# Attention scan, Fourier mixing and two MLPs on one core: the mixing works inside the tile of keys and queries

## The chip, the cores and the metric

One core of a Trainium2 chip runs the whole program. The metric is the device time of one execution in microseconds (us), as a median over runs.

## The reference

For each of 4 images (the batch), 8 heads, 768 positions and a head width of 48, an attention with a complex decaying state is computed, its real part is the image X (768 positions by 384 features), and two MLP blocks follow:

```
for t in range(S):
    S = a_n[t] * S + k[t] v[t]^T          # complex S, a_n = a scaled to |a| <= 0.999
    y[t] = q[t] @ real(S)
u  = X + real(fft(fft(X, axis=positions), axis=features))
un = (u - mean(u)) / sqrt(var(u) + 1e-6)  # per position
u  = u + relu(un @ w_ch1) @ w_ch2         # 384 -> 1536 -> 384
u  = u + (relu(u.T @ w_tok1) @ w_tok2).T  # 768 -> 256 -> 768
out = u + relu(u @ w_ch1') @ w_ch2'       # 384 -> 1536 -> 384
```

## The kernel before

Work on an image b falls into a **chain** (`stage1` and `stage2`) and a **dense** part (the MLPs). The chain of image b+1 runs beside the dense part of image b, so that for b = 0 there is no dense work to run beside, and the chains of images 1, 2 and 3 lie over the dense parts of images 0, 1 and 2. After the chain of image 3 only dense work is left.

- **Scan.** The decay products of the positions are built (DVE, ACT, POOL), and keys and queries, scaled by them, are transposed on PE and copied by ACT (`st_t`, L463 and L641) into a tile `qkt` of 112 partitions by 12288 columns: 64 column groups of 96 for the keys, 64 for the queries. The group of head h and chunk c is h*8+c.
- **Chunks.** The 768 positions are handled in 8 chunks of 96. For chunk c, `ch_load` (L747) fetches the values V and the plain keys Kn, `ch_sc` (L756) makes the masked scores (PE L761, DVE L768), `ch_u` (L771) advances the state: PE L776 and L777, then DVE L787 (Aa), DVE L793, POOL L794 and L795, and DVE L797 (T). `ch_y` (L802) makes the output (PE L810 from scores and values, PE L816 from queries and T), and ACT (L818) puts it into `xT`, 96 columns a chunk. The state update of chunk c-1 gives the T that L816 of chunk c reads; the last update is that issued in chunk 6.
- **Mixing** (`stage2`, L968). It takes a second tile `ws` out of the same pool slot as `qkt` (one buffer), so it begins when the last reader of `qkt` is done. The columns of `ws` are shared out by the table `WSP` (L964). *Folds* (L996) subtract and add column n and column 384+n of `xT`, DVE the difference and POOL the sum; L1002 adds and subtracts halves of these. The table `XP` (L38) says in which column pieces: for b > 0 the pieces are 288 and 96 columns wide. *Mirrors* (L1013) combine column n with column 384-n, with two one-column copies on ACT (L1020, `NR` L39 is the range). Then come a transform over the features (PE L1036, evicted by ACT L1038 into `Z`, first kt = 0 and then kt = 1, four kinds each), the transform over the positions (PE L1047, ACT L1055, L1056 and L1083, POOL L1084 and L1085), transposes (PE L1094) and a join with X (DVE L1099) into `u`, mean and variance (L1106 and L1107), and the normalisation (L1115 to L1122, ACT L1126 writes `un`).
- **Dense.** `transposed` (L907) transposes `un` on PE (L914) and splits it into a high and a low part (ACT L917, DVE L918); `mlp` (L921) runs PE L934 (first matrix), ACT L938 (relu, high part), DVE L947 or ACT L944 and POOL L945 (low part), PE L956 (second matrix) and DVE L959 (adds to `u`). The token MLP is L1145, L1146, L1161, L1167, L1168, L1179 and L1181. For b = 0 the weights are split into high and low parts in the free time of the chain (`tick`: DVE L194, POOL L196, DVE L199, ACT L205, POOL L206).

The order on each engine is set ahead of time: a scheduler plays the program through on a modelled timeline, and where several instructions could go next it takes the one of the better rank. The ranks (`RANK`, L60) put the chain before the dense part on PE, and the dense part before the chain on DVE. The engines then run their lists strictly in this order. The fold of b = 0 is tied by hand to the ticks of chunks 5 and 6.

## Time and profile before

| | before |
|---|---|
| runs | 1093.06, 1094.05, 1094.24 us (median 1094.05) |
| the profiled execution | 1093.5 us; span of its records 1091.7 us |
| PE busy | 978.8 us (90%) |
| DVE / ACT / POOL busy | 769.3 / 511.1 / 417.9 us |
| mean granted clock of PE | 0.966 |

Time is read against the span: 1.8 us of the profiled execution lie outside it. A row of a timeline gives a start, a length, an engine, a line, what is written from what is read, and a count; brackets at its end say how long the engine had been idle before it and what ended that. Rows of neighbouring instructions of one line are taken together, and their lengths overlap a little on PE. A share of busy time over the whole span says little here, since stages differ: the first 180 us are the chain of image 0 alone, the last 260 us are dense work alone.

### The profile page before, as it was taken

The numbers are of one execution on the slowest core, as the hardware profiler recorded it, in microseconds if no ns is written. First come the engines' busy times: TensorE is split into PE (matmuls) and PEld (weight loads), VectorE is DVE, ScalarE is ACT, GpSimd is POOL, SyncE is SP. The second block draws the span as 40 slices with busy tenths as digits, with TensorE's granted clock in tenths as the row PEclk, the third lists the DMA queues.
The fourth block names the chain that finished last, engine by engine and source line by source line (L and its number), as shares of the span: only waits on it lengthen the run. The fifth ranks groups of instructions, "written<-read, shape, count | busy, mean of one in ns | idle before, by whom it ended". The sixth has DMA issues, their size and how long they took to land.

```text
span 1091.7 us, 21067 instructions
## 1 busy us (share of the span) xinstructions
PE 978.8 (90%) x7314; PEld 915.3 (84%) x7314; DVE 769.3 (70%) x2083; ACT 511.1 (47%) x1425; POOL 417.9 (38%) x541
## 2 busy tenths in 40 slices
PE   1567788999899988999998999999897999999997
PEld 0337766989788986899997899999787999999997
DVE  6988887999999678999658879974734433433332
ACT  6753446777875236877216556842224112121111
POOL 6625994673676454345336312424512002000000
PEclk9988896999999999899999999999998999999999
DMA  6238943776668563465575345665303434543432
GB/s 219 48 101 233 290 165 118 252 264 206 200 235 270 162 180 113 117 184 175 156 198 148 100 139 187 203 165 132 128 17 117 146 114 135 159 156 127 163 101 76
DMA packets 101537, 174.66 MB, mean 160 GB/s; under 512 B 11056, under 2 KB 61104, under 8 KB 100912
## 3 DMA queue, kind: packets, MB, share of 16 engines
q1 hardware_dynamic: 101424, 173.24, 51.5%
q8 instruction: 60, 0.98, 0.4%
q14 instruction: 53, 0.43, 0.1%
HBM read 133.88 MB, written 39.32 MB: 159 GB/s over the span
## 4 chain that ended last, share of the span: by engine, by line
PE 68%; DVE 16%; DMA 6%; POOL 4%; ACT 3%; issue 2%; SPq 0%; POOLq 0%; DVEq 0%; ACTq 0%
PE l L956 24%; PE l L934 23%; PE s L761 4%; DMA cvt<-wL 3%; PE s L650 2%; PE s L1047 2%; PE s L810 2%; DVE cvt L199 2%; DVE ws L1002 2%; PE s L1036 1%; PE s L816 1%; PE s L1161 1%; POOL cvt L196 1%; DVE ws L996 1%; PE s L1179 1%
## 5 line engine op out<-in xcount | busy, mean ns | idle before, releaser
L956 PE MATMUL l<-w,h 128*128 128x384 f32 x1728 | 326.5, 339 | 6.8 <-DVE h L947 4.0
L934 PE MATMUL l<-th,w 128*128 128x384 f32 x1152 | 316.0, 344 | 8.8 <-DVE h L947 4.3
L956 PEld LDWEIGHTS l<-w,h 128*128 128x128 f32 x1728 | 297.2, 188 | 11.1 <-DVE h L947 6.3
L934 PEld LDWEIGHTS l<-th,w 128*128 128x128 f32 x1152 | 213.1, 191 | 12.2 <-DVE h L947 6.1
L934 PE MATMUL l<-tl,w 128*128 128x384 f32 x576 | 196.3, 341 | 3.6 <-DVE tl L918 3.6
L938 ACT ACTIVATE h<-l 128x384 fp32r<-128x384 f32 x192 | 94.1, 490 | 213.2 <-PE l L934 212.7
L959 DVE TENSOR_TENSOR u<-u,l 128x384 f32<-128x384 f32 x192 | 105.3, 549 | 83.1 <-PE l L956 82.4
L947 DVE SCALAR_TENSOR_TENSOR h<-l,h 128x384 fp32r<-128x384 f32 x160 | 88.5, 553 | 91.0 <-ACT h L938 90.8
L934 PEld LDWEIGHTS l<-tl,w 128*128 128x128 f32 x576 | 110.3, 191 | 4.2 <-DVE tl L918 4.2
L196 POOL TENSOR_TENSOR cvt<-cvt 128x384 int32<-128x384 int32 x56 | 66.3, 1190 | 38.3 <-DVE cvt L194 7.3
L761 PE MATMUL s<-qkt 112*96 112x96 f32 x512 | 57.8, 263 | 11.0 <-DVE sc L768 11.0
L472 PE MATMUL s<-misc,y 128*112 128x128 f32 x96 | 22.2, 379 | 47.3 <-DVE y L450 44.5
L761 PEld LDWEIGHTS s<-qkt 112*96 112x96 f32 x512 | 51.8, 173 | 13.8 <-DVE sc L768 12.0
L472 PEld LDWEIGHTS s<-misc,y 128*112 128x112 f32 x96 | 14.8, 183 | 57.0 <-POOL tm L366 19.1
L1146 POOL TENSOR_TENSOR xl<-u,xh 128x384 fp32r<-128x384 f32 x18 | 17.9, 1005 | 107.1 <-ACT xh L1145 107.1
L206 POOL TENSOR_TENSOR w<-cvt,w 128x384 fp32r<-128x384 f32 x44 | 52.2, 1197 | 8.3 <-ACT w L205 8.0
L199 DVE SCALAR_TENSOR_TENSOR cvt<-cvt 128x384 int32<-128x384 int32 x56 | 45.9, 828 | 5.9 <-POOL cvt L196 5.8
L579 POOL TENSOR_TENSOR tm<-tm 128x144 f32<-128x144 f32 (+1 forms) x51 | 26.8, 526 | 58.9 <-ACT tm L578 58.6
L945 POOL TENSOR_TENSOR h<-full,h 128x384 fp32r<-128x384 f32 x32 | 33.8, 1057 | 37.2 <-ACT full L944 35.4
L623 DVE TENSOR_TENSOR p<-p,A 128x144 f32<-128x144 f32 x144 | 44.6, 310 | 2.1
L650 PE MATMUL s<-misc,y 128*112 128x128 f32 x288 | 45.2, 276 | 0.9 <-DVE y L634 0.3
L794 POOL TENSOR_TENSOR yc<-Aa,gm 48x384 f32<-48x384 f32 x18 | 21.0, 1164 | 62.4 <-DVE Aa L787 62.4
(232 smaller groups left out, 1940.8 us busy)
## 6 DMA issues: line engine op xcount, KB each, us to landing
w<-wscr SPq DMA_DIRECT2D x180, 384.0 KB, 3.4
cvt<-wL SPq DMA_DIRECT2D x56, 384.0 KB, 5.0
wscr<-w SPq DMA_DIRECT2D x44, 384.0 KB, 3.7
Kn<-kn SPq DMA_DIRECT2D x64, 192.0 KB, 3.7
kn<-y SPq DMA_DIRECT2D x96, 96.0 KB, 2.6
raw<-aL SPq DMA_DIRECT2D x48, 144.0 KB, 3.1
xx<-xL SPq DMA_DIRECT2D x48, 144.0 KB, 2.9
V<-vL SPq DMA_DIRECT2D x32, 144.0 KB, 3.2
```

The source lines that it names most:

```text
L196: x = ge.tensor_tensor(out=a, in0=a, in1=lo, op=ALU.add)
L199: rest(ve.scalar_tensor_tensor(out=a, in0=hi, scalar=-0x80000000, in1=a, op0=ALU.bitwise_and, op1=ALU.bitwise_or))
L206: ge.tensor_tensor(out=parts[:, 1, :], in0=a.bitcast(F32), in1=r32(parts[:, 0, :]), op=ALU.subtract)
L472: te.transpose(ps[:, j, :], y[:, j, 0:112], ident)
L623: ve.tensor_tensor(out=cur, in0=prev, in1=A[:, j, 0:3, :], op=ALU.mult)
L650: te.transpose(ps[:, j, :], y[:, j, 0:112], ident)
L761: te.matmul(out=ps[:, j, :], lhsT=K[:, hc, :], rhs=Q[:, hc, :])
L934: te.matmul(out=ps, lhsT=w1[:, wi, kt * 128:kt * 128 + 128], rhs=x[g][:, kt, :], start=(n == 0), stop=(n == 8))
L938: x = se.activation(out=hi, in_=ps, func=ACTF.Relu)
L947: ve.scalar_tensor_tensor(out=lo, in0=ps, scalar=0.0, in1=r32(hi), op0=ALU.max, op1=ALU.subtract)
L956: te.matmul(out=ps, lhsT=hs[m][:, hi, tt * 128:tt * 128 + 128], rhs=w2[:, wi, :], start=(n == 0), stop=(n == 8))
L959: ve.tensor_tensor(out=u[tt], in0=u[tt], in1=ps, op=ALU.add)
```

## The change

- `qkt` has 128 partitions and its column groups are ordered by chunk: c*8+h for h*8+c. The ACT copies of `st_t` write the same elements in a pattern of one more dimension; `ch_sc` and `ch_y` index accordingly. So the columns of a chunk's keys lie together, and so do those of its queries.
- `stage2` no longer takes a tile of its own: it works in `qkt` (that of b = 0 too, whose folds lay in other tiles before), and its instructions wait for the readers of just the columns that they overwrite. `WSP` puts the halves of the folds (`xd`) over the keys of chunks 0 to 3, the mirrors (`fd`) after it, the folds over queries. Folds are stored closely packed, a piece at a time.
- For b > 0 the pieces of the folds are 192, 96 and 96 columns. The first needs the chunks 0, 1, 4 and 5, the second also 2 and 6, the third also 3 and 7.
- The mirrors are done in two ranges, columns 97 to 192 and then 0 to 96. The order is: folds but the last, mirrors 97 to 192, `dft(1)` (the transform over features with kt = 1), last fold, mirrors 0 to 96, for b = 0 the ticks, `dft(0)`. Only the last fold, its mirrors and `dft(0)` depend on chunk 7.
- For each b > 0 DVE has one fold, three halves and six mirrors more, POOL one fold, one half and two mirrors more, of smaller tiles and the same elements in all; b = 0 has eight more mirrors on DVE.
- `ch_load` of chunk 7 no longer fetches the plain keys, which nothing read (two transfers an image).

```diff
...
 AH = 4
 KS, EN = 5, 3
 OFF = ((2, 3), 1, 0)
-XP = [((0, 96), (96, 96), (192, 96), (288, 96))] + [((0, 288), (288, 96))] * 4
-NR = [((0, 192),)] * 5
-KT, PF, PD = (0, 1), ((2, 0), (2, 1)), (((1, 0), (1, 1)), ((1, 1),))
+XP = [((0, 96), (96, 96), (192, 96), (288, 96))] + [((0, 192), (192, 96), (288, 96))] * 4
+NR = ((97, 192), (0, 96))
+PF, PD = ((2, 0), (2, 1)), (((1, 0), (1, 1)), ((1, 1),))
 O = (0, 1, 0)
 HOLD = mybir.DependencyInfo(mybir.DependencyClass.NoSync, mybir.DependencyReason.SCHED_ONLY)
 CHK_A, CHK_E = 6.0e4, 1.0e-7
...
 
         def st_t(i, k):
             if not qk:
-                qk.append(alloc("qk", [112, 12288], name="qkt").rearrange("p (k g s) -> p k g s", k=2, g=64))
-            qkt = qk[0]
+                qk.append(alloc("qk", [128, 12288], name="qkt"))
+            qkt = qk[0][0:112]
             d = t[i]
             s0 = d["s0"]
             y = ybuf[k][i % 2]
             ps = palloc("s", [112, N4, 128])
             for j in range(N4):
                 te.transpose(ps[:, j, :], y[:, j, 0:112], ident)
-            src = ps.rearrange("p s (g c) -> p g c s", g=2)
+
+            def rows(ap, o, step, g=()):
+                return with_ap(ap, o, [*g, (96, 8), (768, 8), (step, N4)])
+
+            def cols(o, g=()):
+                return with_ap(ps, o, [*g, (8, 8), (1, 8), (128, N4)])
             if k == 0:
-                se.copy(out=with_ap(qkt, s0, [(64 * 96 + 48, 2), (96, 64), (1, N4)]), in_=src)
+                se.copy(out=rows(qkt, s0, 1, [(64 * 96 + 48, 2)]), in_=cols(0, [(64, 2)]))
             else:
-                se.copy(out=with_ap(qkt, 64 * 96 + 47 - s0, [(96, 64), (-1, N4)]), in_=src[:, 0])
-                se.copy(out=qkt[:, 0, :, 48 + s0:48 + N4 + s0], in_=src[:, 1])
+                se.copy(out=rows(qkt, 64 * 96 + 47 - s0, -1), in_=cols(0))
+                se.copy(out=rows(qkt, 48 + s0, 1), in_=cols(64))
 
         def st_end():
 
...
             ve.tensor_scalar(out=gate[:, b:b + 1], in0=fl, scalar1=127.5, scalar2=None, op0=ALU.is_ge)
 
         st = {}
+
+        def halves():
+            v = qk[0][0:112].rearrange("p (k g s) -> p k g s", k=2, g=64)
+            return v[:, 0], v[:, 1]
         PU = "l" if b == 0 else "s"
 
         def ch_load(c):
             v = alloc("P", [96, 384], name="V")
             sp.dma_start(out=v, in_=vL[b, c])
+            st[c] = dict(v=v)
+            if c == 7:
+                return
             kt = alloc("A", [96, 8, 128], name="Kn")
             for hf in range(2):
                 sp.dma_start(out=kt[48 * hf:48 * hf + 48],
                              in_=knd[hf].rearrange("(h c) s f -> c s h f", c=8)[c])
-            st[c] = dict(v=v, kt=kt)
+            st[c]["kt"] = kt
 
         def ch_sc(c, half):
             ps = palloc("s", [96, 4, 96])
-            Q, K = qk[0][:, 1], qk[0][:, 0]
+            K, Q = halves()
             for j in range(4):
-                hc = (half * 4 + j) * 8 + c
+                hc = c * 8 + half * 4 + j
                 te.matmul(out=ps[:, j, :], lhsT=K[:, hc, :], rhs=Q[:, hc, :])
             sc = alloc("e", [96, 4, 96], name="sc")
             mb = mask.unsqueeze(1).to_broadcast([96, 4, 96])
...
 
         def ch_y(c):
             d = st[c]
-            Q = qk[0][:, 1]
+            Q = halves()[1]
             ps = palloc(PU, [112, 4, 96])
             for p in range(4):
                 for k in range(2):
...
                         h = 2 * p + k
                         m = 48 if k else 64
                         te.matmul(out=ps[64 * k:64 * k + m, p, :], lhsT=st["T"][:, h * 48:h * 48 + m],
-                                  rhs=Q[:, h * 8 + c, :], start=False, stop=True)
+                                  rhs=Q[:, c * 8 + h, :], start=False, stop=True)
             marked(se.activation(out=xT[:, :, c * 96:c * 96 + 96], in_=ps, func=ACTF.Copy, scale=gate[0:112, b:b + 1]))
 
         if b == 0:
...
             if b == 0 and c < 7:
                 rests[0], rests[1] = tops[c], st["yop"]
                 tick(CF[c + 1], c == 5)
+        return qk[0]
 
 
     def fallback(b):
...
                     done(tt)
 
 
-    WSP = {"xf": (0, 3072), "Z": (0, 1552), "xr": (1552, 1536), "fd": (3088, 3088), "cb": (3088, 1737),
-           "xd": (6176, 3072), "un": (6176, 2304), "smat": (9248, 2048), "cc": (4825, 1158)}
+    WSP = {"xd": (0, 3072), "fd": (3072, 3088), "xf": (6160, 3072), "Z": (6160, 1552), "xr": (7712, 1536),
+           "smat": (9248, 2048), "cb": (0, 1737), "cc": (1737, 1158), "un": (3072, 2304)}
     ZK = ((128, 64), (128, 64), (128, 65), (128, 63))
 
-    def stage2(b):
-        space = alloc("qk", [128, 12288], name="ws")
+    def stage2(b, space):
         def part(name, pat=None, **kw):
             o, n = WSP[name]
             v = space[:, o:o + n]
...
         u = [alloc("u", [128, 384], name=f"u{i}") for i in range(6)]
 
 
-        if b == 0:
-
-            xm, xp = (alloc("h", [112, 4, 384], name="xf") for _ in range(2))
-            xd = alloc("h", [112, 4, 384], name="xd")
-            xd = [[xd[:, 0:2], xd[:, 2:4]], [alloc("tmp", [112, 2, 384], name="xd") for _ in range(2)]]
-        else:
-            xf = part("xf", "p (a b) -> p a b", a=8)[0:112]
-            xm, xp = xf[:, 0:4, :], xf[:, 4:8, :]
-            xd = part("xd", "p (s r a b) -> p s r a b", s=2, r=2, a=2)[0:112]
-            xd = [[xd[:, s, r] for r in range(2)] for s in range(2)]
+        xd = part("xd", "p (s r a b) -> p s r a b", s=2, r=2, a=2)[0:112]
+        xd = [[xd[:, s, r] for r in range(2)] for s in range(2)]
         fd = part("fd", "p (t r a b) -> p t r a b", t=4, r=2, a=2)[0:112]
         Z = part("Z", "p (a b) -> p a b", a=8)
-        for k, (o, n) in enumerate(XP[b]):
+        kinds = ((0, 0, ALU.subtract, 0, 191), (1, 0, ALU.add, 1, 192), (2, 1, ALU.add, 0, 192), (3, 1, ALU.subtract, 1, 191))
+
+        def folds(k, o, n):
+            at = WSP["xf"][0] + 8 * o
+            x = space[0:112, at:at + 8 * n].rearrange("p (a b) -> p a b", a=8)
             n += o
             an = None if b or AN[k] is None else free[AN[k]]
-            for s, x, op in ((0, xm, ALU.subtract), (1, xp, ALU.add)):
-                x1 = (ge if s else ve).tensor_tensor(out=x[:, :, o:n], in0=xT[:, :, o:n], in1=xT[:, :, 384 + o:384 + n], op=op)
+            for s, op in ((0, ALU.subtract), (1, ALU.add)):
+                y = x[:, 4 * s:4 * s + 4]
+                x1 = (ge if s else ve).tensor_tensor(out=y, in0=xT[:, :, o:n], in1=xT[:, :, 384 + o:384 + n], op=op)
                 if an is not None:
                     after(x1, an)
                 if b == 0 and k == 3 and s == 0:
-                    warm(1, xm[:, 0, :])
+                    warm(1, y[:, 0, :])
                 for r, op2 in enumerate((ALU.add, ALU.subtract)):
-                    x1 = (ge if (s, r) in PD[b > 0] else ve).tensor_tensor(out=xd[s][r][:, :, o:n], in0=x[:, 0:2, o:n], in1=x[:, 2:4, o:n], op=op2)
+                    x1 = (ge if (s, r) in PD[b > 0] else ve).tensor_tensor(out=xd[s][r][:, :, o:n], in0=y[:, 0:2], in1=y[:, 2:4], op=op2)
                     if an is not None:
                         after(x1, an)
                     if b == 0 and k == 3 and s == 0:
                         warm(1, xd[0][r][:, 0, :])
 
-        kinds = ((0, 0, ALU.subtract, 0, 191), (1, 0, ALU.add, 1, 192), (2, 1, ALU.add, 0, 192), (3, 1, ALU.subtract, 1, 191))
-        for n0, n1 in NR[b]:
+        def mirrors(n0, n1):
             for ty, s, op, f0, f1 in kinds:
                 lo, hi, sh = max(n0, f0, 1), min(n1, f1, 191) + 1, ty % 2
                 for r in range(2):
                     x = (ge if (ty, r) in PF and b else ve).tensor_tensor(out=fd[:, ty, r, :, lo - sh:hi - sh], in0=xd[s][r][:, :, lo:hi],
                                                                 in1=xd[s][r][:, :, 384 - lo:384 - hi:-1], op=op)
-                    if b == 0 and ty < 2:
+                    if b == 0 and ty < 2 and not n0:
                         warm(1, fd[:, ty, r, 0, 1:191])
                 for n in (0, 192):
                     if n0 <= n <= n1 and f0 <= n <= f1:
                         for r in range(2):
                             se.copy(out=fd[:, ty, r, :, n - sh:n - sh + 1], in_=xd[s][r][:, :, n:n + 1])
-
-        if b == 0:
-            marked(x)
-            rests[0], rests[1] = x, None
-            for _ in range(5):
-                tick(0)
-            rests[0] = None
-
-
-        for kt in KT:
+            return x
+
+        def dft(kt):
             for ty in range(4):
                 n0, n = 128 * kt, ZK[ty][kt]
                 ps = palloc("s", [128, 2, 97])
...
                         te.matmul(out=ps[0:n, r, :], lhsT=fd[:, ty, r, dt, n0:n0 + n], rhs=dcos[0:112, ty % 2, dt, r, :],
                                   start=(dt == 0), stop=(dt == 1))
                 se.copy(out=Z[0:n, 2 * ty + kt, :].rearrange("p (i r) -> p r i", r=2), in_=ps[0:n])
+
+        for k, (o, n) in enumerate(XP[b][:-1]):
+            folds(k, o, n)
+        mirrors(*NR[0])
+        dft(1)
+        folds(len(XP[b]) - 1, *XP[b][-1])
+        x = mirrors(*NR[1])
+        if b == 0:
+            marked(x)
+            rests[0], rests[1] = x, None
+            for _ in range(5):
+                tick(0)
+            rests[0] = None
+        dft(0)
 
         if b == 0 and WZ:
             warm(WZ, ident)
...
         return f(*args)
 
     def chain(b):
-        stage1(b)
-        return stage2(b)
+        return stage2(b, stage1(b))
 
     sp.dma_start(out=dcos, in_=cD)
     sp.dma_start(out=fk, in_=cFk)
...
     with tc.If(fv != 0):
         with tc.For_i(0, B, 1) as b:
             fallback(b)
-            u, norm = stage2(B)
+            u, norm = stage2(B, alloc("qk", [128, 12288], name="ws"))
             t = transposed(u, norm, "s")
             dense2(B, u, *dense1(B, u, *t), row=b)
 
```

The second `st_t`, for b > 0, is changed in the same way. In the lists that follow, the new kernel's lines are its own: L787 is L804, L793 to L797 are L810 to L814, L768 is L785, L934 is L952, L945 is L963, L947 is L965, L956 is L974, L959 is L977, L914 is L932, L917/L918 is L935/L936, L996 is L1010, L1002 is L1016, L1013 is L1026, L1047 is L1067, L1094 is L1114, L1099 is L1119 and L1161 is L1181.

DVE's list at the end of the chunks of image 3 (u is the dense part's sum; Aa, Xx and T belong to the state update of chunk 6; ws and qkt are the workspace), before:

```order
L787 TENSOR_TENSOR Aa<-T,s 112x384
L793 TENSOR_TENSOR Xx<-Aa,gm_82 112x384
L797 TENSOR_TENSOR T<-Xx,yc_79 112x384
L768 TENSOR_TENSOR sc<-s,misc 96x384 x2
L959 TENSOR_TENSOR u_6497<-u_6497,l 128x384
L996 TENSOR_TENSOR ws<-xT 112x4x288
L996 TENSOR_TENSOR ws<-xT 112x4x96
L959 TENSOR_TENSOR u_6498<-u_6498,l 128x384
L1002 TENSOR_TENSOR ws<-ws 112x2x288 x2
```

And of the changed kernel:

```order
L1010 TENSOR_TENSOR qkt<-xT 112x768
L804 TENSOR_TENSOR Aa<-T,s 112x384
L1016 TENSOR_TENSOR qkt<-qkt 112x2x192 x2
L810 TENSOR_TENSOR Xx<-Aa,gm_82 112x384
L1016 TENSOR_TENSOR qkt<-qkt 112x2x192
L977 TENSOR_TENSOR u_6499<-u_6499,l 128x384
L814 TENSOR_TENSOR T<-Xx,yc_79 112x384
L785 TENSOR_TENSOR sc<-s,misc 96x384 x2
L977 TENSOR_TENSOR u_6500<-u_6500,l 128x384
L1010 TENSOR_TENSOR qkt<-xT 112x384
L1016 TENSOR_TENSOR qkt<-qkt 112x2x96 x3
L1026 TENSOR_TENSOR qkt<-qkt 112x2x95 x6
```

All folds stood behind the last scores; now the fold of 768 elements stands ahead of the state update of chunk 6 and its halves (112x2x192) among it, and the second piece with its mirrors ahead of the third.

POOL's list at the same place (yc is its part of the state update, h the low part of the dense relu), before:

```order
L794 TENSOR_TENSOR yc_79<-Aa,gm_82 48x384
L795 TENSOR_TENSOR yc_79<-Aa,gm_82 48x384
L996 TENSOR_TENSOR ws<-xT 112x4x288
L996 TENSOR_TENSOR ws<-xT 112x4x96
L1002 TENSOR_TENSOR ws<-ws 112x2x288
L1002 TENSOR_TENSOR ws<-ws 112x2x96
L945 TENSOR_TENSOR h<-full,h 128x384
```

And of the changed kernel:

```order
L811 TENSOR_TENSOR yc_80<-Aa,gm_82 48x384
L812 TENSOR_TENSOR yc_80<-Aa,gm_82 48x384
L1010 TENSOR_TENSOR qkt<-xT 112x768
L811 TENSOR_TENSOR yc_79<-Aa,gm_82 48x384
L812 TENSOR_TENSOR yc_79<-Aa,gm_82 48x384
L1016 TENSOR_TENSOR qkt<-qkt 112x2x192
L1010 TENSOR_TENSOR qkt<-xT 112x384
L1016 TENSOR_TENSOR qkt<-qkt 112x2x96
```

POOL's fold of the first piece now stands ahead of its two instructions of chunk 6's state update.

PE's list at the end of image 3's mixing, from the last part of the transform over positions to the token MLP of image 3 (the dense part is that of image 2 up to L956, un of image 3 is in ws or qkt), before:

```order
L1047 MATMUL s<-ws 128x193
L1094 MATMUL s<-misc,xT 128x112 x4
L1094 MATMUL s<-misc,ws 128x112 x4
L956 MATMUL l<-w,h 128x384 x9
L914 MATMUL s<-misc,ws 128x128 x18
L1161 MATMUL s<-xh,w 128x384 x10
```

And of the changed kernel:

```order
L952 MATMUL l<-th,w 128x384 x2
L952 MATMUL l<-tl,w 128x384
L952 MATMUL l<-th,w 128x384
L974 MATMUL l<-w,h 128x384 x6
L932 MATMUL s<-misc,qkt 128x128 x3
L974 MATMUL l<-w,h 128x384 x12
L932 MATMUL s<-misc,qkt 128x128 x6
L974 MATMUL l<-w,h 128x384 x18
L932 MATMUL s<-misc,qkt 128x128 x3
L974 MATMUL l<-w,h 128x384 x18
L932 MATMUL s<-misc,qkt 128x128 x6
L1181 MATMUL s<-xh,w 128x384 x10
```

Behind the last L1094 stood nine matmuls of dense work and then the 18 transposes of `un`; now 10 matmuls of L952 (the list shows the last four) and 54 of L974 stand behind it, and the transposes are spread among them.

## Rows read from the trace of the kernel before

**Rows 1.** The page, busy time of each engine.

```profile
PE 978.8 (90%) x7314; PEld 915.3 (84%) x7314; DVE 769.3 (70%) x2083; ACT 511.1 (47%) x1425; POOL 417.9 (38%) x541
```

**Rows 2.** Windows: stretch, length, busy us (instructions) of PE, PEld, DVE, ACT, POOL, clock, DMA.

```profile
397.00:444.00 47.00, 35.50 (x215) 29.03 (x212) 41.85 (x124) 28.39 (x89) 23.19 (x32) 0.89 0.42 131
444.00:577.00 133.00, 133.00 (x1211) 127.92 (x1210) 105.08 (x323) 74.21 (x224) 55.41 (x82) 0.99 0.59 170
577.00:592.00 15.00, 10.39 (x65) 9.79 (x61) 14.84 (x17) 7.94 (x22) 13.38 (x10) 0.89 0.66 194
775.00:789.00 14.00, 10.42 (x68) 9.36 (x64) 13.23 (x12) 3.54 (x8) 11.47 (x7) 0.99 0.54 188
822.00:834.00 12.00, 5.16 (x23) 4.62 (x24) 6.99 (x16) 6.33 (x16) 5.76 (x6) 0.72 0.23 85
```

**Rows 3.** Timeline of PE, images 1 to 3, the long waits.

```profile
404.69 1.86 PE L956 MATMUL l<-w,h 128*128 128x384 f32 x9 [3.02 <-DVE h L947]
...
583.47 0.45 PE L934 MATMUL l<-tl,w 128*128 128x384 f32 x1 [3.58 <-DVE tl L918]
...
787.18 0.44 PE L934 MATMUL l<-th,w 128*128 128x384 f32 x1 [3.17 <-DVE u L959]
...
829.91 1.54 PE L914 MATMUL s<-misc,ws 128*128 128x128 f32 x6 [6.34 <-ACT ws L1126]
```

**Rows 4.** Timeline of DVE and POOL, image 0, end of its folds.

```profile
138.27 6.20 DVE L1013 TENSOR_TENSOR ws<-xd 112x382 f32<-112x382 f32 x8
...
144.82 8.25 POOL L196 TENSOR_TENSOR cvt<-cvt 128x384 int32<-128x384 int32 x6 [2.16 <-DVE cvt L194]
...
161.92 0.52 POOL L1084 TENSOR_TENSOR ws<-ws 128x193 f32<-128x193 f32 x1
```

**Rows 5.** Timeline of ACT, DVE and POOL, image 1, chunk 6 and the folds.

```profile
390.11 0.58 ACT L818 ACTIVATE xT<-s,gate 112x384 f32<-112x384 f32 x1 [1.18 <-PE s L816]
...
391.03 0.55 DVE L787 TENSOR_TENSOR Aa<-T,s 112x384 f32<-112x384 f32 x1 [1.15 <-PE s L777]
...
391.73 1.15 POOL L794 TENSOR_TENSOR yc<-Aa,gm 48x384 f32<-48x384 f32 x1 [3.83 <-DVE Aa L787]
...
393.82 0.56 DVE L797 TENSOR_TENSOR T<-Xx,yc 112x384 f32<-112x384 f32 x1 [1.65 <-POOL yc L795]
...
397.50 3.82 POOL L996 TENSOR_TENSOR ws<-xT 112x1152 f32<-112x1152 f32 x1 [3.71 <-PE s L816]
...
398.71 3.03 DVE L996 TENSOR_TENSOR ws<-xT 112x384 f32<-112x384 f32 x1
```

**Rows 6.** Groups by form, all images (columns as in the page's list of groups).

```profile
L996 DVE TENSOR_TENSOR ws<-xT 112x1152 f32<-112x1152 f32 x3 | 4.1, 1358 | 3.4 <-PE s L816 3.4
L959 DVE TENSOR_TENSOR u<-u,l 128x384 f32<-128x384 f32 x192 | 105.3, 549 | 83.1 <-PE l L956 82.4
```

**Rows 7.** Timelines of image 1 behind the folds: last mirrors, last eviction.

```profile
412.02 1.35 DVE L1013 TENSOR_TENSOR ws<-ws 112x382 f32<-112x382 f32 x2
...
420.52 0.32 ACT L1038 COPY ws<-s 63x194 f32<-63x194 f32 x1
```

**Rows 8.** Windows behind two of PE's waits (columns as in rows 2).

```profile
583.50:586.00 2.50, 2.50 (x9) 2.50 (x10) 2.50 (x3) 0.80 (x3) 2.50 (x3) 0.58 0.78 183
...
830.00:834.00 4.00, 4.00 (x17) 3.90 (x18) 1.11 (x2) 1.41 (x3) 0.00 (x0) 0.62 0.02 4
```

**Rows 9.** Timelines of PE and ACT: a run of L956 in image 1, then the end of image 3's mixing.

```profile
398.39 3.28 PE L956 MATMUL l<-w,h 128*128 128x384 f32 x18
...
818.98 0.64 PE L1094 MATMUL s<-misc,ws 112*128 112x112 f32 x4
819.39 1.81 PE L956 MATMUL l<-w,h 128*128 128x384 f32 x9
...
831.10 2.91 PE L1161 MATMUL s<-xh,w 128*128 128x384 f32 x10
...
829.15 1.30 ACT L1126 ACTIVATE ws<-u,rs 128x384 f32<-128x384 f32 x2 [3.05 <-DVE rs L1122]
```

More of the change, by code (lines that the diff above doesn't have):

```diff
@@ L642, in st_t @@
             if not qk:
-                qk.append(alloc("qk", [112, 12288], name="qkt").rearrange("p (k g s) -> p k g s", k=2, g=64))
-            qkt = qk[0]
+                qk.append(alloc("qk", [128, 12288], name="qkt"))
+            qkt = qk[0][0:112]
             d = t[i]
```

11 lines of the change are left out of this document (7 added, 4 removed).

## Prediction

> **What bounds the kernel now.** I read the page first: PE is busy for 978.8 us of the span of 1091.7 us [rows 1], so the kernel can only become faster where PE waits or where its clock is low. Then windows by stage: in 444 to 577 us, chunks beside dense work, PE has no gap at all. The gaps sit where the chain runs out of cover, at each image's mixing: 11.5 us of 47 for image 1, 4.6 of 15 for image 2, 3.6 of 14 at the folds of image 3, and 6.8 of 12 before its token MLP [rows 2]. The page by lines would hide this, since the same lines run gapless in other stages. Third, PE's timeline names the long waits. Three stand behind the folds: 3.02 us for L947, 3.58 for L918, 3.17 for L959 [rows 3]; none of these is a fold. They are small dense instructions of DVE that stand in its list behind folds. The fourth, 6.34 us, is for `un` of image 3 [rows 3].
>
> Why the folds hold DVE is in the form and in the neighbour. The first fold, 1152 elements, takes 1.36 us on DVE; the second, a third of it, takes 3.03 us, while POOL's fold of 1152 runs for 3.82 us beside it [rows 5, 6]. L959, which reads one operand from PSUM, is steady at 0.55 us beside anything [rows 6]. So folds on DVE and POOL pass through one gate in turn, whichever came first. The Trainium skill, SBUF — State Buffer, section "Who interferes with whom", has this as a rule: a DVE instruction with two SBUF inputs contends with a GpSimd instruction that reads SBUF, and the one that issued first blocks the other for its whole length. By it, work moved forward beside POOL's does not become free, it blocks what stands behind it; that is the slow rival below, and rows 5 bear the rule out for the folds themselves.
>
> **The change, part by part.** All sums go against the profiled execution, 1093.5 us; the median of the runs, 1094.05, lies 0.55 above it.
>
> *Layout and the copies of the scan.* The ACT copies write the same elements, in one dimension more. No row of before shows that pattern. Nothing speaks for a gain, and ACT is busy for 511.1 of 1091.7 us [rows 1], so I take nothing; if each of the 180 copies took a tenth of a microsecond more, 18 us spread over four scans would have to fit into 580 us of idle ACT. The two transfers a chunk that go are off SP's queue in the last chunk, where nobody waits for them: nothing.
>
> *Image 0, later by 1.2 us.* The mirrors become 16 halves for 8 wholes, which now take 6.20 us [rows 4]. The same elements, eight fixed costs more; two forms give the size of one: 1152 elements in 1.36 us against L959's 384 in 0.55 [rows 6] are 0.81 us for 768 elements, so 0.40 for 384, which leaves about 0.15 us a piece, together 1.2. POOL's conversions start right behind the mirrors (L196 at 144.82), and the mixing's L1084 stands behind their whole queue, at 161.92 [rows 4], so the delay passes to the mixing, which here has no dense work beside it. The split also lets `dft(1)` go early, but `dft(0)` is behind the ticks as before. Bounds: 0, if the shorter pieces slip between POOL's, and 2.5, if each pays double beside POOL.
>
> *Image 1, nothing.* The fold of 768 elements moves ahead of chunk 6's state update. By rows 5 and 6 it costs DVE 0.9 us alone and POOL 2.5 (3.82 by two thirds). POOL sat idle for 3.83 us before L794 [rows 5], but not at the right time: chunk 5's output is in `xT` at 390.69, 0.34 us before L787 [rows 5], so the fold fills the time in which L794 and L795 ran. On DVE three halves of 384 elements stand between L787 and L797 as well. I put chunk 6's T later by POOL's 2.5 us and some 0.6 for halves that wait in turn: 3.1 us. What is saved behind chunk 7 is these same instructions, 4 to 5 us, so that the 3.02 us wait shrinks; but PE gets to chunk 7's end 3 us later. At the other end `Z` is complete with the last L1038 at 420.52 [rows 7]. With kt = 1 first only 12 matmuls remain behind the last mirrors at 413.37 [rows 7], yet in the new list the last L1038 stands behind three more scan instructions of image 2. I let these cancel. Bounds: -4 (all of the wait and the end of the mixing move up) and +3 (T's delay uncovered).
>
> *Image 2, later by 2.5 us.* Here the output of chunk 7 has only six transposes L914 ahead of it as cover when T is late by 3.1 us, so some 2.5 of them reach PE. The wait of 3.58 us for L918 [rows 3] shrinks as the folds leave, but L947 in the new list comes only after all mirrors 97 to 192 and the last fold. Its low clock, 0.58 behind the wait [rows 8], stays as it is. Bounds: -3 and +5.
>
> *Image 3, earlier by 7 us.* This is the change's one large effect, and it is in PE's list: 64 dense matmuls stand behind the last L1094, where nine stood. Eighteen of L956 take 3.28 us, nine 1.81 [rows 9], so 64 are some 11 us, against 9.2 us from the end of the last L1094 (819.62) to `un` at about 829 [rows 9, 3]. The 6.34 us then hold work, and the short waits around it too: 6.8 us idle in this window. PE's clock at 0.62 behind it for 4 us [rows 8] costs some 1.2 us more, since the ten L1161 take 2.91 us there. That makes 8. Against it: the 55 matmuls come from somewhere earlier, between chunk 7 and L1047, where they covered the folds; with T late by 3.1 and a thinner cover I give 1 us back. Bounds: -9, all of it and half the wait of 3.17 at the folds, and -2, where the earlier stage takes most of it back.
>
> Sum: 1.2 + 0 + 2.5 - 7 = -3.3 us, 1090.2 in the profiled execution, 1090.8 as a median.
>
> **The rivals.**
> - *The early folds are free.* Chunk 6 leaves POOL idle for 3.83 us and DVE for 1.15 and 1.65 [rows 5]; if the folds fall into these, T is not late, and the waits behind chunk 7 go: image 1 gives 3.5, image 2 gives 3, image 3 all 7.4. With 1.2 lost, 12.7 together: 1081.4. For it: dense matmuls cover PE without a gap through all of chunk 6. Against it: the order of the lists.
> - *The early folds stand before T in all three images (the other side).* The place is DVE's and POOL's list ahead of chunk 6's L797; the price is 3.1 us an image. It decides from the point where fewer than about 18 dense matmuls (3.28 us [rows 9]) stand on PE between chunk 7's scores and its outputs. Then 9.3 + 1.2 - 7 = 3.5 later: 1097.6. For it: rows 5, and image 2 has six transposes there. Against it: PE's new list for image 3 has 13 dense matmuls between the scores and chunk 6's outputs, and six more before chunk 7's, which first read this T.
> - *It only moves.* The gate between DVE and POOL has as many elements to pass as before; if each mixing ends when the last element has passed, image 3's gap opens again, earlier, where the 55 matmuls were taken. About 1094, within 2. That the change does not do what it says belongs here: an ACT list that puts the edge copies ahead of chunk 7's output, as it does, ties that output to the mirrors it was to run beside.
>
> **How the numbers follow.** My forecast, a gain that is mostly image 3's, between 1087 and 1093, has a chance of 0.42; free folds 0.20; T late everywhere 0.16; only moved 0.22. A measurement here tells 0.2%, about 2.2 us, from no change. Faster (under 1091.9): 0.36 of the forecast's 0.42 and the 0.20, 0.56. Same: the rest of the forecast and most of what only moves, 0.24. Slower: 0.20. The range for 8 in 10 goes from 1083, inside the free folds, to 1098, past T late. By sign most of the chance is on faster; the likeliest case alone spans 1087 to 1093.
>
> **What would show it.** Right: PE's wait of 6.34 us before L1161 is gone and L1181 (its new line) starts about 65 dense matmuls behind the last L1114; POOL's L811 of chunk 6 begins 2 to 3 us after Aa in place of 0.2 us; in image 2 a wait of PE before chunk 7's outputs. Wrong: chunk 6's T as soon after Aa as now (2.8 us), which would be the first rival; a new wait of PE between chunk 7 and the first L1067 of image 3 of over 4 us, which would be the third; image 0's first L1104 more than 2.5 us later; an ACT copy of the scan clearly longer than now with PE waiting behind it.

## The result, and the profile after

The changed kernel takes 1080.94 us (median of 4 runs, 1079.18 to 1081.88) beside 1094.14 us of the kernel before (4 runs too): a ratio of 0.9875, with a 95% interval of 0.9855 to 0.9895. It is 13.2 us faster. The forecast was 1090.8 with a range from 1083, so the sign was right and the size wrong. The time is that of the first rival, 1081.4; its mechanism, as will be seen, is not.

The profiled execution took 1079.18 us, span 1077.4. The page's first section, after [rows 1]:

```profile
PE 979.0 (91%) x7314; PEld 915.2 (85%) x7314; DVE 773.1 (72%) x2121; ACT 511.9 (48%) x1425; POOL 415.1 (39%) x553
```

PE's busy time is the same to 0.2 us, so the gain is time in which PE waited. To see where, I cut both traces at the same places of the program: first L1161 of image 0, first L1161 of image 1, end of image 2's last L1094, first L1161 of image 2 (it stands behind image 3's mixing; the lists ahead of the prediction call it image 3's token MLP, but it is image 2's), end. Windows of before, columns as in [rows 2]:

```profile
0.00:268.30 268.30, 195.84 (x1434) 167.16 (x1435) 227.79 (x645) 164.53 (x459) 167.52 (x212) 0.92 0.60 188
268.30:536.10 267.80, 248.14 (x1935) 231.26 (x1934) 232.92 (x683) 167.71 (x490) 137.84 (x184) 0.97 0.60 180
536.10:621.30 85.20, 80.58 (x850) 72.89 (x849) 61.79 (x151) 31.75 (x95) 36.47 (x45) 0.98 0.52 147
621.30:831.10 209.80, 199.30 (x1625) 189.54 (x1625) 151.08 (x434) 101.00 (x288) 69.98 (x95) 0.98 0.47 140
831.10:1091.70 260.60, 254.98 (x1478) 254.40 (x1476) 95.76 (x174) 46.12 (x96) 6.07 (x6) 0.99 0.40 131
```

Windows of after, cut at the same places:

```profile
0.00:269.40 269.40, 199.03 (x1435) 170.11 (x1436) 230.31 (x654) 165.71 (x459) 166.40 (x212) 0.90 0.59 186
269.40:534.30 264.90, 246.95 (x1926) 229.48 (x1925) 234.74 (x690) 166.94 (x490) 136.79 (x188) 0.98 0.60 182
534.30:618.20 83.90, 80.91 (x847) 72.99 (x847) 62.84 (x160) 32.11 (x94) 35.48 (x48) 0.96 0.48 141
618.20:817.60 199.40, 198.12 (x1637) 189.22 (x1635) 149.07 (x447) 100.41 (x287) 67.58 (x98) 1.00 0.48 140
817.60:1077.40 259.80, 254.02 (x1479) 253.44 (x1476) 96.12 (x175) 46.72 (x98) 8.84 (x9) 1.00 0.42 136
```

The stages differ by +1.1, -2.9, -1.3, -10.4 and -0.8 us: -14.3 in these two executions. A second profiled execution of the changed kernel (`after_beside`) gives +3.0, +0.8, -3.8, -10.1 and -1.0, so only the fourth, the stage that holds image 3's chunks and mixing, moves by clearly more than two executions of one kernel differ. It is most of the gain. There PE's idle time falls from 10.5 us (209.80 less 199.30) to 1.3, and the clock rises from 0.98 to 1.00.

PE's timeline of after holds the waits that answer to [rows 3], one in each image, now ahead of chunk 7's outputs (L827), and the end of image 3's mixing, which answers to [rows 9]:

```profile
400.71 0.38 PE L827 MATMUL s<-sc,V 96*64 96x96 f32 x4 [1.31 <-DVE sc L785]
...
577.17 1.01 PE L932 MATMUL l<-misc,u 128*128 128x128 f32 x6 [2.56 <-DVE tl L936]
...
771.79 0.37 PE L827 MATMUL s<-sc,V 96*64 96x96 f32 x4 [1.28 <-issue]
...
810.33 3.39 PE L974 MATMUL l<-w,h 128*128 128x384 f32 x18
813.56 0.49 PE L932 MATMUL s<-misc,qkt 128*128 128x128 f32 x3
813.80 3.37 PE L974 MATMUL l<-w,h 128*128 128x384 f32 x18
817.01 0.82 PE L932 MATMUL s<-misc,qkt 128*128 128x128 f32 x6
817.58 0.59 PE L1181 MATMUL s<-xh,w 128*128 128x384 f32 x2
```

No row from the last L1114 to L1181 has a bracket: the 6.34 us are filled. DVE's and POOL's timelines of after, chunk 6 of image 3, answer to [rows 5]:

```profile
764.58 0.55 DVE L804 TENSOR_TENSOR Aa<-T,s 112x384 f32<-112x384 f32 x1
765.04 2.84 DVE L1016 TENSOR_TENSOR qkt<-qkt 112x384 f32<-112x384 f32 x2
767.81 1.19 DVE L810 TENSOR_TENSOR Xx<-Aa,gm 112x384 f32<-112x384 f32 x1
...
770.68 0.54 DVE L814 TENSOR_TENSOR T<-Xx,yc 112x384 f32<-112x384 f32 x1
...
763.80 2.54 POOL L1010 TENSOR_TENSOR qkt<-xT 112x768 f32<-112x768 f32 x1 [2.94 <-issue]
766.42 1.05 POOL L811 TENSOR_TENSOR yc<-Aa,gm 48x384 f32<-48x384 f32 x1
```

From the start of Aa to that of T it is 6.1 us, where it was 2.8 [rows 5], the same in all three images; in images 1 and 2 it is now 5.7 and 6.6. So the early fold does make T late, by 2.9, 3.8 and 3.3 us (forecast 3.1). The two halves L1016 take 1.4 us each beside POOL's fold and its L811, and L810 1.19 in place of 0.56: what the Trainium skill says of two SBUF inputs (SBUF — State Buffer, "Who interferes with whom") agrees. But PE pays little for it: 1.3, 3.0 (2.56 and 0.43) and 1.3 us. What ends the first two is not T itself but its neighbours in DVE's list, L785 behind it and L936 ahead of it; what ends the third, the profile does not name.

### The profile page after: what moved, and what is told of

Same layout as the page of the kernel before. It is cut to its first block, busy times and chain, and to the rows that moved or that the text cites. A ratio compares the mean times of both kernels' runs of the same rounds, so it can differ in the third digit from the quotient of the medians.

```text
span 1077.4 us, 21129 instructions
## 1 busy us (share of the span) xinstructions
PE 979.0 (91%) x7314; PEld 915.2 (85%) x7314; DVE 773.1 (72%) x2121; ACT 511.9 (48%) x1425; POOL 415.1 (39%) x553
## 4 chain that ended last, share of the span: by engine, by line
PE 65%; DVE 18%; POOL 5%; issue 4%; DMA 4%; ACT 3%; SPq 0%; DVEq 0%; POOLq 0%; ACTq 0%
PE l L974 24%; PE l L952 23%; PE s L778 3%; PE s L655 2%; DMA cvt<-wL 2%; DVE cvt L199 2%; PE s L827 2%; POOL cvt L196 1%; PE s L1067 1%; PE s L1042 1%; POOL w L206 1%; PE s L833 1%; PE s L1181 1%; PE s L1199 1%; PE s L793 1%
## 5 line engine op out<-in xcount | busy, mean ns | idle before, releaser
L974 PE MATMUL l<-w,h 128*128 128x384 f32 x1728 | 326.1, 339 | 4.4 <-DVE h L965 2.9
L952 PE MATMUL l<-th,w 128*128 128x384 f32 x1152 | 316.3, 344 | 5.2 <-DVE h L965 4.2
L974 PEld LDWEIGHTS l<-w,h 128*128 128x128 f32 x1728 | 297.1, 188 | 8.8 <-DVE h L965 5.3
L952 PEld LDWEIGHTS l<-th,w 128*128 128x128 f32 x1152 | 212.5, 191 | 8.6 <-DVE h L965 6.3
L952 PE MATMUL l<-tl,w 128*128 128x384 f32 x576 | 196.1, 341 | 0.0
L956 ACT ACTIVATE h<-l 128x384 fp32r<-128x384 f32 x192 | 94.4, 492 | 211.9 <-PE l L952 211.4
L977 DVE TENSOR_TENSOR u<-u,l 128x384 f32<-128x384 f32 x192 | 105.2, 549 | 69.7 <-PE l L974 69.2
L965 DVE SCALAR_TENSOR_TENSOR h<-l,h 128x384 fp32r<-128x384 f32 x160 | 88.5, 554 | 89.6 <-ACT h L956 89.4
L952 PEld LDWEIGHTS l<-tl,w 128*128 128x128 f32 x576 | 110.0, 191 | 0.3 <-DVE tl L936 0.3
L196 POOL TENSOR_TENSOR cvt<-cvt 128x384 int32<-128x384 int32 x56 | 66.0, 1185 | 43.3 <-DVE cvt L194 10.4
L811 POOL TENSOR_TENSOR yc<-Aa,gm 48x384 f32<-48x384 f32 x18 | 20.6, 1145 | 65.9 <-DVE Aa L804 65.6
L602 POOL TENSOR_TENSOR A<-raw,tm 128x144 f32<-128x144 f32 (+1 forms) x51 | 26.5, 519 | 47.4 <-DVE tm L600 28.5
```

Source lines behind the costliest of these rows:

```text
L196: x = ge.tensor_tensor(out=a, in0=a, in1=lo, op=ALU.add)
L952: te.matmul(out=ps, lhsT=w1[:, wi, kt * 128:kt * 128 + 128], rhs=x[g][:, kt, :], start=(n == 0), stop=(n == 8))
L956: x = se.activation(out=hi, in_=ps, func=ACTF.Relu)
L965: ve.scalar_tensor_tensor(out=lo, in0=ps, scalar=0.0, in1=r32(hi), op0=ALU.max, op1=ALU.subtract)
L974: te.matmul(out=ps, lhsT=hs[m][:, hi, tt * 128:tt * 128 + 128], rhs=w2[:, wi, :], start=(n == 0), stop=(n == 8))
L977: ve.tensor_tensor(out=u[tt], in0=u[tt], in1=ps, op=ALU.add)
```

## Experiments

Two questions stood first: which part of the change carries the gain, and how much of it is PE's list. Behind image 3's last transposes stood 9 dense matmuls before and stand 64 now, and a variant changes this number without meaning to, since the scheduler lays all lists anew. So for each kernel its number is told.

**The first fold late** (`late_first_fold`):

```diff
-XP = [...] + [((0, 192), (192, 96), (288, 96))] * 4
+XP = [...] + [((0, 288), (288, 96))] * 4
```

> The changed kernel with the fold pieces of before for images 1 to 3 (288 and 96 columns): the first fold then needs chunk 6 and no fold stands ahead of chunk 6's T. The shared tile, the split mirrors and the early half transform stay. Theory 'cover' (the gain of image 3 is the dense work that PE's list has left behind the last transposes; PE's list has 32 such matmuls here, 9 before, 64 in the changed kernel): the idle time there is 6.9 us less 23 times 0.173, about 2.9, so image 3 keeps some 6 of its 11 us, images 1 and 2 half of their 4; about 1086 to 1088. Rival 'split' (the split mirrors and the early half transform carry the gain, the early fold only makes T late): T is 3 us earlier and nothing is lost, 1079 to 1081.

Measured: 1094.81 us, ratio 1.0001 (0.9985 to 1.0017). Nothing of the gain is left; both theories missed. PE's timeline of this kernel, images 1, 2 and 3:

```profile
407.61 0.52 PE L1042 MATMUL s<-dcos,qkt 112*64 112x97 f32 x4 [2.45 <-DVE qkt L1026]
...
590.12 1.63 PE L1042 MATMUL s<-dcos,qkt 112*64 112x97 f32 x8 [6.35 <-DVE qkt L1026]
...
788.31 0.85 PE L1042 MATMUL s<-dcos,qkt 112*64 112x97 f32 x8 [2.41 <-DVE qkt L1026]
...
830.74 0.48 PE L932 MATMUL s<-misc,qkt 128*128 128x128 f32 x1 [3.75 <-ACT qkt L1146]
```

The fourth wait is near what 32 matmuls should leave (2.9 expected). The first three are what I had not counted: the early half transform, which the scheduler now puts forward on PE, waits for mirrors whose folds begin only with chunk 6's output.

**Folds late, mirrors whole, shared tile** (`whole_mirrors`): the same table, and for images 1 to 3

```diff
-mirrors(*NR[0]); dft(1); folds(last piece); x = mirrors(*NR[1]); dft(0)
+folds(last piece); x = mirrors(0, 192); dft(0); dft(1)
```

> The changed kernel with, for images 1 to 3, the fold pieces of before, the mirrors whole and the transform over features in the old order, all in the shared tile; image 0 stays as in the changed kernel. Theory 'cover': 17 dense matmuls are left behind the last transposes of image 3, so the gap before the token MLP is still some 5.5 us; the folds of chunk 7 stall DVE as before; with image 0's 1.1 us about 1091 to 1094. Rival 'tile' (the shared tile alone, with no wait for the release of all of it, brings the gain): 1081 to 1084.

Measured: 1098.27 us, 1.0034 (1.002 to 1.0048). The shared tile alone brings nothing; rival "tile" falls. The 3 us more than before are not explained by the wait for `un` (6.88 us, 17 matmuls, where it was 6.34).

**Image 0 whole** (`image0_whole`): the same edit for b = 0 alone.

> The changed kernel with image 0's mirrors as eight wholes and its transform in the old order; images 1 to 3 unchanged. Theory 'pieces' (the eight more instructions of DVE delay POOL's conversions and through them image 0's mixing): 1.1 us less than the changed kernel, 1079.8. Rival (the delay of image 0 comes from the folds' new place in the shared tile or from the copies of the scan): no change, 1080.9.

Measured: 1080.23 us, 0.9875 (0.984 to 0.991): undecided. In its profile the dense work of image 0 begins at 177.28 us and not at 179.74, but the end of the span does not follow: from the token MLP of image 0 to that of image 1 it takes 269.5 us, where the changed kernel took 264.9 in one profiled execution and 268.6 in the other.

**The fold behind T** (`fold_behind_T`), in `folds`, with the two instructions that end chunk 6's state update kept:

```diff
+if 0 < b < B and k == 0:
+    after(x1, last[s])        # order only: s = 0 DVE L814, s = 1 POOL L812
```

> The changed kernel with the first fold of images 1 to 3 tied behind chunk 6's state update on both engines (an order only). T of chunk 6 then comes 2.8 us after Aa as before and not 6.2. Theory 'cover': what T's delay cost PE (waits of 1.3, 3.0 and 1.3 us) comes back, but the folds end later and only 32 dense matmuls are left behind image 3's last transposes, so a gap of about 2.9 us opens there: 1080 to 1084. Rival 'late T' (the delay of T is a plain loss of 5.6 us): 1075 to 1076.

Measured: 1096.66 us, 1.0018 (1.0 to 1.0037). T is on time again (Aa at 778.05, T at 780.85 in image 3), and the whole gain is gone. Behind chunk 7 PE here waits 4.29 us (image 1), 5.01 (image 2) and 3.69 (image 3) again: a fold that stands behind T is dearer than T's delay. How much of the loss is the fold's place alone is not shown, since the list left 32 matmuls at the end, with a wait for `un` of 3.74 us, and was laid anew elsewhere too.

**The layout alone** (`layout_alone`): the kernel before with the new column order, its copies, and without chunk 7's unused transfers.

> The kernel before with only the new column order of keys and queries, the copies of the scan that it needs, and without chunk 7's two unused transfers; the mixing keeps a tile of its own, folds and mirrors as before. Both theories: no change against before, 1093 to 1096 (PE's list has no dense matmul behind the last transposes of image 3, nine before, so up to 1.5 us more). A copy of the scan that is slower in the new pattern would show as a longer scan of image 0.

Measured: 1100.64 us, 1.0062 (1.0041 to 1.0084), slower than expected. The scan's copies are not the cause: 587, 356 and 374 ns in image 0 (medians), where they took 585, 354 and 374. Image 3's end waits longer, with no dense matmul in the list:

```profile
829.69 1.54 PE L931 MATMUL s<-misc,ws 128*128 128x128 f32 x6 [4.73 <-ACT ws L1143]
833.49 0.90 PE L931 MATMUL s<-misc,ws 128*128 128x128 f32 x3 [2.26 <-ACT ws L1143]
...
824.00:838.00 14.00, 6.78 (x25) 5.79 (x26) 8.70 (x25) 7.88 (x17) 5.77 (x6) 0.52 0.00 1
```

The last row is the window around it: clock 0.52. It is not the whole: in the profiled execution, 4.8 us longer than that of before, image 2's last transposes already end 2.6 us later (623.87 us for 621.27), and the stage of image 3 is 1.0 us longer. That the lists came out otherwise is the likely reason of the 6 us; no run shows it.

**The early fold for image 3 alone** (`image3_early`): images 1 and 2 have the pieces 288 and 96.

> The changed kernel with the early 192-column fold piece for image 3 alone; images 1 and 2 have the pieces of 288 and 96 columns. Theory 'early piece' (each image gains by itself what its own folds have moved ahead of chunk 7's output): images 1 and 2 as in the run with the late first fold, some 4 us behind before by image 2's transposes, then image 3's 10 to 11 us: 1085 to 1089. Rival 'list' (the gain hangs on one lucky order of PE's list, which needs all three images as they are): 1092 to 1095.

Measured: 1089.0 us, 0.9964 (0.9947 to 0.9982), at the upper end. Images gain apart; rival "list" in this form falls.

**Early fold, whole mirrors** (`early_fold_whole_mirrors`): the new table with the edit of `whole_mirrors`.

> The changed kernel with its early fold piece, but for images 1 to 3 the mirrors whole, behind the last fold, and the transform over features in the old order. Theory 'early piece': the folds are most of what was moved, half or more of the gain stays: 1083 to 1088. Rival 'both' (the early fold pays only together with the mirrors 97 to 192, since DVE and POOL still have 5 us of mirrors behind the last fold and 17 dense matmuls are left for image 3's end): 1089 to 1093.

Measured: 1094.58 us, 1.0 (0.9984 to 1.0016). No gain, less than both theories gave. Its wait for `un` is 6.88 us.

**Both halves of the first fold on DVE** (`first_fold_on_DVE`):

```diff
-x1 = (ge if s else ve).tensor_tensor(out=y, ...
+x1 = (ge if s and (b == 0 or b == B or k) else ve).tensor_tensor(out=y, ...
```

> The changed kernel with both halves of the early 192-column fold on DVE for images 1 to 3, so that POOL has nothing ahead of chunk 6's L811. If DVE and POOL exclude each other, T of chunk 6 comes some 1 to 2 us earlier after the fold, and Aa 1 us later. Theory 'early piece': as the changed kernel or 1 to 2 us better, 1079 to 1081, although PE's list has only 14 dense matmuls behind image 3's last transposes (64 in the changed kernel). Rival 'cover' (what counts for image 3 is that dense work left over): a gap of 6 us opens there again, 1085 to 1088.

Measured: 1083.79 us, 0.9912 (0.9881 to 0.9942), between the two. From Aa to T it is 4.8 us in image 3 (768.14 to 772.93), 1.3 less than in the changed kernel, and image 2's wait shrinks to 0.55 us. But its wait for `un` is 6.13 us, with 14 matmuls. So the two effects have opposite signs here, and the next runs show that the second can be taken away.

**The list alone.** The waits for `un` of image 3, from PE's timelines, against the number of dense matmuls in PE's list between the last transposes of image 3 and the token MLP:

| kernel | matmuls | wait for un, us | median, us |
|---|---|---|---|
| layout alone | 0 | 4.73 and 2.26 | 1100.6 |
| before | 9 | 6.34 | 1094.1 |
| first fold on DVE | 14 | 6.13 | 1083.8 |
| early fold, whole mirrors | 17 | 6.88 | 1094.6 |
| late first fold | 32 | 3.75 | 1094.8 |
| fold behind T | 32 | 3.74 | 1096.7 |
| image 3 early | 42 | 1.92 | 1089.0 |
| changed | 64 | none | 1080.9 |

From 17 to 32 to 42 the wait falls by about 0.2 us a matmul, near the 0.18 of one [rows 9]. Up to 17 it does not fall (7.0, 6.3, 6.1 and 6.9 us), which stays open, and the medians do not follow the number alone. The next four runs set the number by an order; in three of them the order is the only change to a kernel of the table. Into `mlp`, with the last transpose L1094 of image 3 kept:

```diff
+if b == B - 2 and done is None and qd == 3 and n == 0:
+    after(x, last[0])         # these L956 behind image 3's last transpose
```

On the kernel before (`before_tail_held`):

> The kernel before with one order added: the last 54 matmuls of L956 of image 2's first MLP stand behind the last transposes of image 3 (55 dense matmuls there, 9 before; none is left beside the transform over positions). Theory 'cover': the wait for un of 6.3 us and the low clock behind it go, some 7 to 8 us; as far as the mixing itself waits on DVE, POOL and ACT for want of those 46 matmuls (8 us), it comes back: 1088 to 1094. If the list is what makes the changed kernel's gain at image 3, it reaches 1088 here without the change. Rival 'chain' (image 3's mixing is as long as its own work on DVE and POOL, whatever PE does beside it): 1093 to 1095, the wait has only moved.

Measured: 1088.67 us, 0.9935 (0.9913 to 0.9958). Rival "chain" falls. PE's timeline of this kernel, image 3's end (L957 is L956, L915 is L914):

```profile
811.82 0.64 PE L1097 MATMUL s<-misc,ws 112*128 112x112 f32 x4
812.23 4.77 PE L957 MATMUL l<-w,h 128*128 128x384 f32 x26
...
817.58 4.96 PE L957 MATMUL l<-w,h 128*128 128x384 f32 x27
...
823.90 0.55 PE L915 MATMUL s<-misc,ws 128*128 128x128 f32 x3 [0.71 <-ACT ws L1131]
825.87 0.55 PE L915 MATMUL s<-misc,ws 128*128 128x128 f32 x3 [1.42 <-DVE tl L919]
```

The mixing needs none of the 46 matmuls beside it: its last transposes come at 811.82 and not at 818.98, and the waits that open behind them are the two shown, 0.71 and 1.42 us, in place of 6.34. The waits at the folds (3.15 us in image 3) stay. So 6 of the change's 13 us were to be had with one order and no change of the mixing.

With the first fold on DVE (`DVE_fold_tail_held`):

> The kernel with the first fold all on DVE, with the same order added (55 dense matmuls behind image 3's last transposes, 14 without it). Theory 'cover': its wait of 6.1 us for un and the low clock behind it go: 1075 to 1078. Rival 'chain': the wait moves to the transform over positions, 1082 to 1085.

Measured: 1078.7 us, 0.9841 (0.9817 to 0.9864): 5.1 us less than without the order, and just above what "cover" gave.

With four pieces of 96 columns (`four_pieces_tail_held`, the table of image 0 for all images):

> The changed kernel with four fold pieces of 96 columns for images 1 to 3, each as soon as its chunk is there (chunks 4 to 7), and the same order added (55 dense matmuls behind image 3's last transposes, 19 without it). If what counts is the work of DVE and POOL behind chunk 7 and the cover at the end, as the changed kernel, with T later by less in two chunks for more in one: 1076 to 1080. If T's delay is paid twice: 1083 to 1086.

Measured: 1078.82 us, 0.9845 (0.9823 to 0.9867), within the first of the two. Here chunk 6's T comes 2.8 us after Aa, as before the change, and chunk 5's 4.3 to 4.7: T need not be as late as in the changed kernel for the gain. PE's idle time from image 1's token MLP to image 2's last transposes is 0.4 us, where the changed kernel has 3.0, and that stage takes 78.8 us in both profiled executions of this kernel, 83.9 and 81.3 in those of the changed one. Image 3's stage gives 1.3 us of it back (200.7 for 199.4).

With the early fold and whole mirrors (`early_fold_whole_tail_held`):

> The run with the early fold and whole mirrors, with the same order added (55 dense matmuls behind image 3's last transposes, 17 without it). Tells what its missing gain was. If it was PE's list: its wait of 6.9 us for un goes, with the clock 8 to 9 us, 1085 to 1087. If it was the whole mirrors behind the last fold: the wait moves ahead of the transform over features, 1092 to 1095.

Measured: 1088.15 us, 0.9936 (0.9914 to 0.9959), 6.4 us less, so that much of its missing gain was the list; the other 7 us, to the changed kernel's 1080.9, are elsewhere. Most of them stand in image 2: from image 1's token MLP to image 2's last transposes this kernel takes 90.7 us, the changed one 83.9 and 81.3. Windows of 30 us over image 2's mixing; the first is this kernel, the second the one with four pieces:

```profile
575.00:605.00 30.00, 25.19 (x150) 23.50 (x149) 22.52 (x50) 16.65 (x53) 13.34 (x19) 0.77 0.43 134
```

```profile
575.00:605.00 30.00, 30.00 (x246) 27.70 (x244) 27.60 (x79) 19.76 (x61) 16.43 (x26) 1.00 0.50 156
```

The missing corners, late folds with split mirrors (`late_fold_tail_held`) and late folds with whole mirrors (`whole_mirrors_tail_held`):

> The run with the late first fold (split mirrors, early half transform), with the order added that leaves 54 dense matmuls behind image 3's last transposes (32 without it). Theory 'cover and split pay apart': the wait of 3.8 us for un and the clock behind it go, 1088 to 1090, and the waits of PE for the mirrors in images 1 to 3 (2.5, 6.4 and 2.4 us) stay: the split without the early fold is worth nothing against the kernel before with the same order (1088.7). Rival (the split is worth its own part once the end is covered): 1083 to 1086.

> The run with late folds and whole mirrors in the shared tile, with the same order (55 dense matmuls behind the last transposes, 17 without it). This is the kernel before with that order but for the shared tile and image 0: its wait of 6.9 us goes, 1089 to 1092. If the shared tile had a cost of its own beyond image 0's 1 us, 1093 to 1096.

Measured: 1092.7 us, 0.9982 (0.9963 to 1.0001), and 1092.75 us, 0.9977 (0.9961 to 0.9994). With 54 or 55 matmuls at the end (the changed kernel has 64 by itself), in the shared tile:

| medians, us | mirrors whole | mirrors split, half transform early |
|---|---|---|
| folds late | 1092.8 | 1092.7 |
| folds early | 1088.2 | 1080.9 (changed kernel) |

The split alone brings nothing, the early fold alone 4.6 us, both 11.9. Each corner's list is laid anew, so a part of each difference may be the list's. The expected 1088 to 1090 for the first was too low, and the second lies between its two; what takes them 4 us above the kernel before with the same order (1088.7) has not been settled. Image 0 is part: its dense work begins at 181.1 and 181.6 us in these two, and at 179.4 there, and by image 0's token MLP the profiled executions are 3.2 and 2.1 us behind, of 2.6 and 3.5 at the end.

**Versions meant to beat both.** Image 0 whole on top (`four_pieces_image0_whole`), and the first two pieces on DVE as well (`four_pieces_DVE`):

> A version meant to beat both: four fold pieces of 96 columns for images 1 to 3, the order that leaves 55 dense matmuls behind image 3's last transposes, and image 0's mirrors whole. If image 0's eight more pieces cost about 1 us: 1077 to 1078, against 1078.8 with them. If not: 1078 to 1079.5.

> As the version before, with the two first fold pieces of images 1 to 3 on DVE alone, so that POOL has no fold ahead of the state updates of chunks 5 and 6. If T's delay still costs PE something in image 2 or 3: 1075 to 1077. If nothing of it is left uncovered with four pieces: 1077 to 1079, since DVE then has more to do.

Measured: 1083.23 us, 0.9887 (0.9849 to 0.9926), and 1086.13 us, 0.9933 (0.9912 to 0.9954). Both medians are above the 1078.82 without the additions, and the clock is where it shows (last section). One of the four runs of the first took 1077.92 us, with the highest granted clock of the four (0.969; the others 0.961 to 0.966), so its loss is not in every execution. Last, the changed kernel and the four pieces with the held order on one chip:

> The changed kernel once more, on one chip with the next one, so that the two can be compared run by run: 1079 to 1082.

> The version with four fold pieces and the order at image 3's end, beside the changed kernel. If its shorter waits in image 2 (0.4 us of idle time in place of 3.0, and no low clock there) count: 2 to 3 us less than the changed kernel, 1077 to 1079. If they are given back elsewhere: within 1 us of it.

Measured: 1079.6 us, 0.9851 (0.9831 to 0.9871), and 1077.83 us, 0.9838 (0.9821 to 0.9855). Four pieces are 1.8 us lower here, and were 2.1 lower in the runs on different chips, with intervals that overlap; that it beats the changed kernel is likely, not shown.

No run takes the 64 matmuls from the changed kernel itself by an order alone; what they are worth is read from the kernel before, from the first fold on DVE and from the early fold with whole mirrors, 6.1, 5.1 and 6.4 us.

## Why the prediction was wrong in size

- **What bounds the kernel: right.** PE's busy time did not move, and the gain is PE's waits in the stages that were named.
- **The copies and the unused transfers at nothing: right** for the copies, whose lengths are the same. That the new layout by itself would be free was wrong: alone it cost 6 us, likely since the lists came out otherwise.
- **Image 0, 1.2 us later: the number came out (268.3 to 269.4), in part by luck**; the second profiled execution has 271.4. The sixteen halves take 7.7 us where the eight wholes took 6.2, and the last of them wait 1.15 us in all for PE's early half transform (L1042). Yet image 0's dense work begins only 0.4 us later (179.74 for 179.32). It begins at 176.5 to 178.0 in the four profiled executions with the new layout and whole mirrors, at 179.6 to 182.7 in all with halves: the halves cost more than forecast, and another part of the change gives some of it back.
- **T later by 3.1 us: right** (2.9, 3.8 and 3.3). **Its price against what the early fold takes away was wrong, in all three images, and this is the step that failed most.** Around the folds PE waited 4.7 us in image 1 (3.02, 0.75 and 0.92), 4.6 in image 2 and 3.6 in image 3 (3.17 and 0.42). I let the two cancel in image 1, let T's delay add 2.5 us in image 2, and in image 3 left the 3.17 us standing and gave 1 back. In the changed kernel PE waits 2.3 us (1.31 and 1.03), 3.0 and 1.3 in their place, the same within 0.3 in its second profiled execution. That is 2.4, 1.6 and 2.3 us less, where the sum had 0 and then 2.5 and 1 more: some 10 of the 11 us by which the forecast missed the first profiled execution (14.3 for 3.3).
- **Image 3, earlier by 7 us: the mechanism right, the term mis-sized:** it was 10.4 us to the token MLP behind it. The 8 us that I put for the wait for `un` and its clock came: 6.9 us of waits went, and PE's busy time there is 1.2 us less. I gave 1 back since "the 55 matmuls come from somewhere earlier, between chunk 7 and L1047, where they covered the folds". They did, but the folds no longer needed them: the 3.17 us wait and 0.42 ahead of it went too, and only 1.28 came. One reading was off, without effect: 829.15 is the start of L1126, so 10.3 us had to be covered and not 9.2; 64 matmuls do for either.
- **The first rival had the time and not the reason.** It said that T is not late; T is as late as in the second, and POOL's L811 begins 1.3 us after Aa has ended in image 3 (0.2 before; I had said 2 to 3). What was right in it is its "for it": dense matmuls cover PE through chunk 6. A delay of 3.3 us there is cheap: it leaves waits of 1.3, 3.0 and 1.3 us, where the fold behind T leaves 4.3, 5.0 and 3.7.
- **The second rival decided where it said it would**, by cover between chunk 7's scores and its outputs: six transposes in image 2 left a wait of 2.56 us, 19 matmuls in image 3 one of 1.28. As a price of the whole change it was wrong.
- **What I did not see at all:** the 64 matmuls are no property of the new mixing. One order gives them to the kernel before (1088.7), and a variant of the change that loses them loses 5 us (1083.8 against 1078.7).

## What to carry to other kernels

Ask of a step that is moved not how late it makes its neighbour but what PE has in its list at the old place and at the new one: microseconds on DVE are cheap under dense matmuls and dear where none are left. Splitting a step and starting its input early can each be worth little and both together much (0.1, 4.6 and 11.9 us here), so take them as one edit. Where a wait at the end of a chain is uncovered, count the independent matmuls that the list has left for it, and try a plain order that saves some: here one order was worth 6 of 13 us.
